# A fused attention and MLP kernel on one core: zeroing moved, dummy matmuls moved to the front, one load freed of a wait, and all written instruction orders replaced

## The chip, the core and the metric

The kernel runs on one core of a Trainium2 chip. Its time is the device time of one execution in microseconds; the figure for a kernel is the median of several executions. The engines are TensorE (PE in the profile, its weight loads PEld), VectorE (DVE), ScalarE (ACT), GpSimd (POOL) and SyncE (SP). Matrix products go to PSUM; a "tile" below is a named buffer in on-chip memory.

## The reference

Eight batches of eight heads, 576 rows, width 64, go through a Nyström approximation of attention with 32 landmarks, and the result through an MLP with a squared ReLU.

```python
q_lm = q.reshape(B, H, m, S // m, D).mean(axis=3)      # m = 32 landmarks
k_lm = k.reshape(B, H, m, S // m, D).mean(axis=3)
A, Bm, C = sm(q, k_lm), sm(q_lm, k_lm), sm(q_lm, k)    # softmax(scale * a @ b.T)
Z = Bm.T / (norm1(Bm) * norminf(Bm) + 1e-6)
for _ in range(6):
    Z = 2 * Z - Z @ Bm @ Z                             # iterative inverse
x = (A @ Z @ C @ v)                                    # to (4608, 512)
out = np.maximum(x @ w_in, 0) ** 2 @ w_out             # w_in 512x2048, w_out 2048x512
```

## The kernel before

The work is done batch by batch. For a batch the kernel copies k and q to bf16 (tile nat), transposes them (T, and tT for the last 64 rows), takes the landmark means as matmuls against a constant matrix seg (L344), puts them on block diagonals (bd), and computes the landmark scores (L374), their softmax (BB), and the iterative inverse as a chain of small products (L416) and VectorE updates (L421). Scores of q and k against the landmarks (L532, with their tails in L560) are exponentiated by ScalarE into EA and EC. EA is normalised (row sums L574, an in L586) and transposed to AT (L598). C times v is gathered in L616. The MLP's first matrix is folded in: G is the small attention factor times w_in (L807), so that the hidden layer h is one product of G with AT (L824); ScalarE applies ReLU (r, L828), VectorE squares (gT, L829), and L853 multiplies by w_out, in 36 tiles of 16 matmuls of 512 columns, followed by copies o_sb and stores.

The first batch, called the head, has no MLP work to hide behind. Its order is the string HEAD; a last product az and its copy AZ stand in for AT there. The other batches are interleaved with the MLP of the batch before, by the eight strings in PLANS: PLANS[b] holds the hidden layer of batch b, the attention of batch b + 1 and output steps. Both are written orders: in the block of `tc.manual_schedule` the instructions of PE, DVE, ACT and SP go out exactly as the tokens say. POOL's order is set by `issue_after` chains and added dependencies.

The tokens that matter here: `ck` casts k to bf16 by halves (VectorE half 0 at L719, ScalarE half 1 at L720) and starts the remaining loads; `tk0`, `tk1`, `tq0`, `tq1` transpose halves, `ek..`, `eq..` copy them out on the engine named by the last letter; `cq0`, `cq1` copy the halves of q; `mk`, `mq` are means; `lm`, `ls` the landmark scores and their softmax; `ib`, `if` begin the inverse, `jo`, `jl`, `nu`, `nn`, `fv` are its steps; `sq`, `sk`, `tl` scores and tails; `sum`, `rec`, `row` normalise EA; `cv`, `cr`, `cba`, `ct` handle C times v; `g:n` makes a quarter of G and `gf`, `gl` copy it out; `w:n:width` issues n dummy matmuls of that width into a tile idle nobody reads (L297, 512 columns without a width), from the zeroed constant bd1. In a plan, `h` is one hidden block, `s` a squaring, a number that many output steps, `pk`, `pq` the copy of k or q of the next batch (L283; with `+` of the batch after it, which starts its transposes on the DMA engines for batches from 3 on), `gg` half of G.

Loads go out from POOL one behind the other (`load`, `behind`), except the first k on SP. `load_rest`, called in `ck`, issues the loads listed in LOADS (parts of w_in, w_out, v, and q and k of batch 1, whose landing place is the tile stage). The first of them is made to wait, through `gate`, for the ScalarE cast of k. Behind these loads POOL copies one part of seg and zeroes two tiles ct, 128 x 1280 bf16 each. ct is read only by batches from DMA_C = 9 on, and there are eight batches; likewise DMA_A = 9 for a transposing DMA of an.

Of the kernel before, what the change touches and what calls it, by code (L numbers as in the profile page):

```python
# [9 lines left out]
P = 128  # L10
# [4 lines left out]
BF16 = mybir.dt.bfloat16  # L15
# [12 lines left out]
NC4 = 4  # L28
# [5 lines left out]
DMA_C = 9  # L34
COMPACT = 1
HEAD = (
    "ck tk1 mk w:1:256 w:1:256 ek1d w:1:256 w:1 tk0 tt w:1 w:1 cq0 cq1 ek0a mq tq0 tq1 lm "
    "w:1 et w:1:256 w:1 eq0a w:1:256 tl eq1d ls sum:0:4:5 w:1 ib w:1 w:1:256 sq1 w:1:256 if "
    "sk1 sum:1:2:5 w:1:256 w:1 sum:1:0:2 jo w:1:256 w:1:256 rec:1 w:1:256 row:1:0:3 "
    "row:1:3:5 w:1:256 sk0 w:1 sq0 jo w:1:256 w:1:256 w:1 w:1:256 sum:0:2:4 sum:0:0:2 w:1 jo "  # L40
    "rec:0 cv:0 cv:1 w:1:256 w:1:256 row:0:3:5 cr jo w:1:256 row:0:0:3 w:1:256 at:1 cba w:1 "
    "jl at:0 ea0d ea1a ct w:1:256 nu w:1:256 g:0 gl1d fv w:1 gf1d w:1 gf0a az gl0d"
)
LOADS = "w10 v0 w00 q1 w01 w11 o0 o1 o2 o3 v1"
PLANS = [
    (
        "pk h g:1 tt h pq h s tk1 s h s h tq1 s tk0 h h mk s s mq tq0 h lm s g:2 g:3 ls sk0 s h "
        "h ib 1 h 1 s if tl h jo 1 sq0 s 1 jo s s 1 h jo 1 sq1 1 jl h 1 nu h s s h nn 2 sk1 nu s "
        "1 s 8 as0 1 ar0 as1 2 ar1 5 nn1 cv 4 wt at0 2 gg0 2 at1 2 gg1 1"
    ),  # L50
    (
        "2 pk 1 h h 1 mk pq s mq 1 s h tq0 lm h ls h tt tq1 3 tl 1 s 1 h ib 1 s if s sq1 2 s h "
        "jo 1 as1 sq0 1 h h s 1 as0 tk1 1 jo 1 s 4 tk0 2 jo 1 h 1 s h 1 pk+ 1 jl ar1 h sk0 1 s 1 "
        "s nu h s 1 sk1 s h h nn s cv nu h 3 nn1 at1 s 3 s wt 3 ar0 2 gg0 3 at0 1 gg1 pq+"
    ),
    (
        "5 mk h 1 h mq s 2 h 5 lm s 2 ls 1 sk1 2 ib 3 h h s sk0 s if 1 s h 2 h 1 jo s h tl 3 jo "
        "1 s 2 h jo 1 s 2 h 3 s sq0 s 1 jl pk+ 4 sq1 2 as0 nu 3 h 1 nn 2 as1 1 pq+ 1 nu 1 h 1 "
        "ar1 h 1 s s h 1 nn1 cv 1 h 2 ar0 1 s wt h 1 at0 2 gg1 1 s at1 1 s 2 gg0 1 s"
    ),  # L60
    (
        "mk 2 h 1 mq 7 h 2 s lm s 1 ls 1 h sq1 1 h h 1 ib 1 s if sk1 1 s h s 2 h jo 1 s 1 h s 1 "
        "jo 2 h 1 pk+ jo 1 tl s h 2 jl as1 sq0 1 s h 1 s h nu s 1 h sk0 s 1 ar1 4 as0 nn 1 ar0 2 "
        "h 3 cv 2 s h nu 4 s nn1 1 at1 1 h wt 2 s 3 s gg1 1 at0 4 gg0 4 pq+"
    ),
    (
        "2 mk h 2 mq 4 h lm 1 h 1 s ls 1 sk0 s ib s 3 h h if 3 tl s 2 h h s 1 s jo 2 h h 1 jo s "
        "1 sq0 s 2 h 1 jo 5 s 10 jl pk+ s 3 sq1 h nu 1 h 1 h 3 as0 sk1 s 1 h 1 as1 ar1 5 s nn cv "
        "nu pq+ 4 s 2 nn1 ar0 h s 4 wt h 2 at0 s 1 gg0 2 s 1 at1 1 gg1 2"
    ),  # L70
    (
        "3 mk mq 3 h lm 3 h h ls 1 s 1 s ib 2 sq1 h 2 if 1 sq0 3 jo h 1 sk0 s jo 2 s h jo tl 4 "
        "as1 1 h 1 jl s sk1 h 3 pk+ s 4 nu h 1 s 2 s 1 s 4 as0 h 1 ar1 nn s 2 ar0 h cv h nu h s "
        "1 s 1 nn1 h 2 h pq+ s wt h 2 at1 2 gg0 at0 5 s 3 s s gg1"
    ),
    (
        "mk 1 mq 3 h s lm 1 h 3 ls 2 h s 1 ib 2 h 1 if sq1 s h 1 s 3 sq0 2 s h 2 s 2 jo h tl 3 "
        "jo 1 h h as0 jo 3 s h 1 s jl 1 s sk1 4 nu 2 as1 h nn 1 h 1 sk0 2 ar0 nu 1 s s 3 h h 1 "
        "cv 2 nn1 s h s 1 at0 1 wt h 2 s 1 ar1 gg0 1 at1 2 s 1 gg1 4 s"
    ),  # L80
    (
        "h 7 h 6 s 1 h 6 h 1 s 2 h s 2 h 6 s 13 h 2 s 2 h 1 s 1 s 5 s h 3 h 1 s s h 11 s 1 h s 8 "
        "h 1 h 1 h 1 s 4 s h 2 s s"
    ),
]

# [2 lines left out]
def kernel(  # L89
# [9 lines left out]
    nc = tc.nc  # L99

    const = ctx.enter_context(tc.tile_pool(name="const", bufs=1))
# [19 lines left out]
    vts, ects, cts = [], [], []  # L121
# [5 lines left out]
        nc.vector.memzero(ect[:])  # L127
        ects.append(ect)

    behind, gate = [], []  # L130

    def load(dst, src, queue=nc.gpsimd):
        with tc.issue_after(behind[0].ins) if behind else nullcontext():
            d = queue.dma_start(dst, src)  # L134
        if gate:
            tc.add_manual_dep(
                d.ins, gate.pop().ins.name,
                mybir.DependencyInfo(mybir.DependencyClass.Sync, mybir.DependencyReason.DATA),
                reason="q first")
        if queue is nc.gpsimd:  # L140
            behind[:] = [d]
        return d
# [18 lines left out]
    def load_qk(b: int, X: dict):  # L161

        X["qkt"] = loads.tile([P, H, D], BF16, tag="qkt", name="qkt")

        def tails():
            for src, r0 in ((k, k_row(b)), (q, q_row(b))):
                load(X["qkt"][r0:r0 + TAIL, :, :],
                     src[b, :, NC4 * P:S, :].rearrange("h p d -> p h d"))

        if b > 0:  # L170
            tails()
        for nm, src in (("k", k), ("q", q)):
            if b < 3:
                X[nm + "raw"] = staged(b, nm)
            else:
                X[nm + "raw"] = loads.tile([P, H, NC4, D], BF16, tag="raw", name="raw")
            parts = ((0, H // 2), (H // 2, H)) if b == 0 and nm == "q" else ((0, H),)
            for lo, hi in parts:
                one = load(
                    X[nm + "raw"][:, lo:hi, :, :],  # L180
                    src[b, lo:hi, 0:NC4 * P, :].rearrange("h (p c) d -> p h c d", c=NC4),
                    nc.sync if b == 0 and nm == "k" else nc.gpsimd)
                if b > 0 and nm + "turn" in loaded[b - 1]:
                    tc.add_manual_dep(
                        one.ins, loaded[b - 1][nm + "turn"].ins.name,
                        mybir.DependencyInfo(mybir.DependencyClass.Sync,
                                             mybir.DependencyReason.DATA),
                        reason="behind the turning of the batch before")
            if b == 0 and nm == "k":
                tails()  # L190

# [10 lines left out]
    loaded = {b: {} for b in range(B)}  # L202
# [6 lines left out]
    seg = const.tile([P, NC4 + 3, M], BF16, name="seg")  # L209
# [21 lines left out]

    EA = const.tile([P, 2, NC4 + 1, P], F32, name="EA")
    nc.vector.memset(EA[:, :, NC4, :], 1.0)

    def load_rest(after):

        def w_in(i, j):
            load(
                w_in_bf[64 * i:64 * i + 64, :, 1024 * j:1024 * j + 1024],
                moe_w_in[256 * i:256 * i + 256, 1024 * j:1024 * j + 1024].rearrange(  # L240
                    "(j d) f -> d j f", d=D),
            )

        def w_out(j):
            load(
                w_out_bf[:, 4 * j:4 * j + 4, :],
                moe_w_out[512 * j:512 * j + 512, :].rearrange("(ft fp) c -> fp ft c", fp=P),
            )

        behind[:] = [masked]  # L250
        gate[:] = [after]
        for x in LOADS.split():
            i = int(x[1])
            if x[0] == "w":
                w_in(i, int(x[2]))
            elif x[0] == "o":
                w_out(i)
            else:
                (load_v if x[0] == "v" else load_qk)(i, loaded[i])
        with tc.issue_after(behind[0].ins):  # L260
            nc.gpsimd.tensor_copy(seg[:, NC4 + 2, :], seg[:, NC4, :])
            for i in range(2):
                ct = const.tile([P, 2, NC4 + 1, P], BF16, name="ct%d" % i)
                nc.gpsimd.memset(ct[:], 0.0)
                cts.append(ct)

    turn = [0]

# [31 lines left out]
    def attention(b: int, R: dict):  # L300

        X = loaded[b]
        BD = bds[b % 2]
        ect = ects[b % 2]
        first = b == 0
# [193 lines left out]
        ct = cts[b % 2] if b >= DMA_C else None  # L499
        c0 = b % 2  # L500
        at = NC4 * (1 - c0)
# [10 lines left out]
        an = attn.tile([P, 2, NC4 + 1, P], BF16, tag="an", bufs=1, name="an")  # L512
        AT = attn.tile([P, 2, (NC4 + 1) * P], BF16, tag="AT", name="AT")
# [76 lines left out]

        def a_transposed(i):
            if b >= DMA_A:
                nc.sync.dma_start_transpose(AT[:, i, :].rearrange("p (c t) -> p c t", t=P),
                                            an[:, i, :, :].rearrange("p c x -> p (c x)"))
                return
            tps = ntile([P, (NC4 + 1) * P], BF16, placed=b > 0)
            for c in range(NC4 + 1):
                nc.tensor.transpose(tps[:, c * P:c * P + P], an[:, i, c, :], ident_bf[:])  # L598
            o = TAIL * c0
            return AT[:, i, o:o + S], tps[:, o:o + S]  # L600
# [110 lines left out]
        def head_step(token):  # L711
# [5 lines left out]
            if name == "ck":  # L717
                raw = natural(0, "k")
                dve(X["k"][:, 0:2], raw[:, 0:2])  # L719
                load_rest(act(X["k"][:, 2:4], raw[:, 2:4]))  # L720
                st["qraw"] = natural(0, "q")
                X["tT"] = attn.tile([P, NPAIR, P], BF16, tag="tT", name="tT")
            elif name[:2] == "cq":
# [252 lines left out]
```

The softmax here doesn't subtract the row's maximum and nothing guards it: scores larger than these inputs give would overflow.

## Time and profile before

| what | value |
|---|---|
| median of 7 runs | 266.14 us (265.54 to 266.64) |
| the profiled execution: time, span | 266.22 us, 264.5 us |
| PE busy | 247.9 us, 94% |
| DVE busy | 176.7 us, 67% |
| ACT busy | 158.3 us, 60% |
| POOL busy | 47.7 us, 18% |
| first PE instruction | 7.67 us |
| first h matmul (L824) | 25.07 us |

The span runs from the first to the last recorded instruction; the profiled execution is 1.72 us longer than it. A row of the timeline reads: start, duration, engine, line, operation, output tile <- input tiles, shapes, count, and in brackets the idle time of the engine before it with what ended it. Matmul records carry the latency of a matmul, so matmuls that follow each other overlap in them.

### The profile page before, as it was taken

The page shows a single profiled execution, that of the slowest core. Times are in us where ns is not written, and L with a number is a line of the kernel's source. Part 1 is how long each engine was busy: PE and PEld are TensorE (multiplying, and loading weights), DVE is VectorE, ACT ScalarE, POOL GpSimd, SP SyncE. Part 2 cuts the span into 40 slices and gives each one's busy share as a digit, 9 for nine tenths or more (in the row PEclk, how much of TensorE's full clock was granted, in tenths as well). Part 3 has the DMA queues.
Part 4 walks back from the last instruction along what each step waited for, and adds up shares of the span by engine and source line. Part 5 has one row for each costly group of instructions (what it writes and reads, how often), then busy time and mean ns, then how long its engine had stood idle before and what let it go on. Part 6 is the DMA issues. An engine that isn't in the chain of part 4 may idle for free.

```text
span 264.5 us, 6918 instructions
## 1 busy us (share of the span) xinstructions
PE 247.9 (94%) x2835; PEld 153.4 (58%) x2878; DVE 176.7 (67%) x485; ACT 158.3 (60%) x278; POOL 47.7 (18%) x73
## 2 busy tenths in 40 slices
PE   0898899999999999999999999999999999999994
PEld 0675665467656656566556565666566655555443
DVE  3488986789985878689767589589776783232100
ACT  2464787279666765678557566674777665365210
POOL 7844633302010500700003101230000000000000
PEclk9999999999999999999999999999999999999999
DMA  8999999997149899996838998999911111112122
GB/s 189 163 192 203 208 206 190 212 208 102 37 95 191 112 194 161 180 205 129 121 79 112 182 184 108 127 176 197 161 51 40 42 40 69 52 40 83 40 79 79
DMA packets 69791, 34.65 MB, mean 131 GB/s; under 512 B 37376, under 2 KB 64256, under 8 KB 69760
## 3 DMA queue, kind: packets, MB, share of 16 engines
q0 software_dynamic: 39808, 17.83, 54.2%
q1 hardware_dynamic: 24704, 7.08, 17.4%
q10 hardware_dynamic: 5248, 9.31, 11.3%
q8 instruction: 22, 0.36, 0.6%
q14 instruction: 9, 0.07, 0.1%
HBM read 36.70 MB, written 9.44 MB: 174 GB/s over the span
## 4 chain that ended last, share of the span: by engine, by line
PE 87%; DVE 5%; DMA 2%; issue 2%; ACT 2%; ACTq 0%
PE ops L853 24%; PE h L824 22%; PE n L853 21%; PE n L532 3%; PE g L807 3%; PE idle L297 2%; DMA stage<-in_k_dram 2%; PE n L416 2%; PE n L344 2%; PE n L598 2%; PE n L616 1%; DVE nat L283 1%; DVE gT L829 1%; PE tps L315 1%; PE n L631 1%
## 5 line engine op out<-in xcount | busy, mean ns | idle before, releaser
L828 ACT ACTIVATE r<-h 128x576 bf16<-128x576 f32 x128 | 81.2, 651 | 46.7 <-PE h L824 33.9
L853 PE MATMUL ops<-w_out_bf,gT 128*128 128x512 bf16 (+1 forms) x300 | 76.8, 368 | 0.9 <-issue 0.3
L853 PEld LDWEIGHTS <-gT 128*128 128x128 bf16 x592 | 53.2, 98 | 38.7 <-issue 4.2
L829 DVE TENSOR_TENSOR gT<-r 128x576 bf16<-128x576 bf16 x128 | 54.8, 447 | 26.3 <-ACT r L828 26.1
L824 PE MATMUL h<-AT,G 128*128 128x288 bf16 x448 | 71.0, 286 | 0.2
L853 PE MATMUL n<-w_out_bf,gT 128*128 128x512 bf16 x252 | 69.7, 379 | 1.1 <-issue 0.3
L824 PEld LDWEIGHTS <-G 128*128 128x128 bf16 x512 | 47.7, 97 | 24.3 <-issue 0.8
L705 DVE CAST G<-g 128x1024 bf16<-128x1024 f32 x14 | 17.1, 1224 | 5.4 <-PE g L807 5.4
L864 ACT COPY o_sb<-ops 128x512 f32<-128x512 f32 (+1 forms) x19 | 10.9, 574 | 14.5 <-PE ops L853 14.5
L864 ACT COPY o_sb<-n 128x512 f32<-128x512 f32 x17 | 10.0, 586 | 12.9 <-PE n L853 12.8
L705 ACT CAST G<-g 128x1024 bf16<-128x1024 f32 x14 | 14.2, 1014 | 4.5 <-PE g L807 4.5
L134 POOL DMA_DIRECT2D raw<-in_k_dram x5 | 4.5, 890 | 54.2 <-DVE gT L829 28.4
L532 PEld LDWEIGHTS <-T 128*128 128x128 bf16 x256 | 11.3, 98 | 4.2 <-issue 0.6
L574 DVE TENSOR_REDUCE ra<-EA 128x20 f32<-128x640 f32 (+3 forms) x19 | 13.2, 703 | 0.3 <-ACT EA L562 0.3
L586 DVE TENSOR_TENSOR an<-EA,rra 128x640 bf16<-128x640 f32 (+2 forms) x18 | 13.2, 736 | 0.2
L532 PE MATMUL n<-bd,T 128*128 128x64 bf16 x256 | 12.7, 193 | 0.3 <-issue 0.2
L315 PEld LDWEIGHTS <-nat 128*128 128x128 bf16 x96 | 6.6, 106 | 9.8 <-ACT nat L720 7.7
L537 ACT ACTIVATE EA<-n 128x512 f32<-128x512 f32 x16 | 9.6, 598 | 3.3 <-PE n L532 3.2
L134 POOL DMA_DIRECT2D raw<-in_q_dram x5 | 4.4, 884 | 38.8 <-DVE rc L447 27.7
L537 ACT ACTIVATE EC<-n 128x512 bf16<-128x512 f32 x16 | 9.5, 596 | 3.0 <-PE n L532 1.6
L824 PE MATMUL h<-AZ,G 128*128 128x288 bf16 x64 | 10.0, 286 | 0.6 <-DVE AZ L797 0.4
L315 PE MATMUL tps<-ident_bf,nat 128*128 128x128 bf16 x32 | 3.1, 266 | 7.7 <-ACT nat L720 7.7
(144 smaller groups left out, 294.8 us busy)
## 6 DMA issues: line engine op xcount, KB each, us to landing
out_dram<-o_sb ACTq DMA_DIRECT2D x31, 256.0 KB, 3.5
vm<-in_v_dram POOLq DMA_DIRECT2D x8, 512.0 KB, 10.2
raw<-in_k_dram POOLq DMA_DIRECT2D x5, 512.0 KB, 6.9
raw<-in_q_dram POOLq DMA_DIRECT2D x5, 512.0 KB, 6.9
w_in_bf<-in_moe_w_in_dram POOLq DMA_DIRECT2D x4, 512.0 KB, 12.3
w_out_bf<-in_moe_w_out_dram POOLq DMA_DIRECT2D x4, 512.0 KB, 17.4
out_dram<-o_sb ACTq DMA_DIRECT2D x9, 128.0 KB, 2.4
stage<-in_k_dram SPq DMA_DIRECT2D x1, 1024.0 KB, 5.7
```

Of the source, the lines that this page charges most:

```text
L134: d = queue.dma_start(dst, src)
L315: nc.tensor.transpose(tps[:, i, p, :], X[nm][:, 2 * half + i, 2 * p:2 * p + 2, :].rearrange("p h d -> p (h d)"), ident_bf[:],)
L532: nc.tensor.matmul(sc[:, c, j, :, :], lhsT=X[nm + "T"][:, c, p, :], rhs=BD[:, 1 if nm == "q" else 0, p, 0:64], start=True, stop=True)
L537: nc.scalar.activation(dst, sc.rearrange("p c j i m -> p c (j i m)"), AF.Exp, scale=SCALE)
L574: nc.vector.reduce_sum(ra[:, quads, lo:hi, :], EA[:, quads, lo:hi, :].rearrange("p q c (h m) -> p q c h m", m=M), axis=AX.X)
L586: on.tensor_tensor(an[:, i, lo:hi, :].rearrange("p c (h m) -> p c h m", m=M), EA[:, i, lo:hi, :].rearrange("p c (h m) -> p c h m", m=M), r ...
L705: (act, dve)[n % 2](G[:, :, n * 512:n * 512 + 512], gg[:])
L824: nc.tensor.matmul(h[:, j, 0:HALF], lhsT=G[:, qd, f * P:(f + 1) * P], rhs=AT[:, qd, a0 + j * HALF:a0 + (j + 1) * HALF], start=(qd == 0), s ...
L828: nc.scalar.activation(r.rearrange("p (j t) -> p j t", j=2), h[:, :, 0:HALF], AF.Relu)
L829: return lambda: nc.vector.tensor_tensor(gT[:, f, o:o + S], r[:], r[:], ALU.mult)
L853: nc.tensor.matmul(ops, lhsT=gT[:, f, t * P:t * P + P], rhs=w_out_bf[:, f, i * n:i * n + n], start=(f == 0), stop=(f == NF - 1))
L864: nc.scalar.copy(o_h, ops)
```

## The change

It does five things. Sixteen dummy matmuls of 512 columns open TensorE's order. ct is zeroed by VectorE at the start, and the part of seg is copied by VectorE too. The wait of the first load of `load_rest` (gate) is taken out. HEAD and all eight PLANS are replaced by new orders of the same steps, with 13 dummies behind the first 16 where there were 35; some steps also change engine (`ek0` from ScalarE to VectorE, `ek1` from VectorE to ScalarE, and so on). A load of k would also wait for the transposing DMAs of `a_transposed` two batches earlier, if there were any.

```diff
 HEAD = (
-    "ck tk1 mk w:1:256 w:1:256 ek1d w:1:256 w:1 tk0 tt w:1 w:1 cq0 cq1 ek0a mq tq0 tq1 lm "
-    "w:1 et w:1:256 w:1 eq0a w:1:256 tl eq1d ls sum:0:4:5 w:1 ib w:1 w:1:256 sq1 w:1:256 if "
-    "sk1 sum:1:2:5 w:1:256 w:1 sum:1:0:2 jo w:1:256 w:1:256 rec:1 w:1:256 row:1:0:3 "
-    "row:1:3:5 w:1:256 sk0 w:1 sq0 jo w:1:256 w:1:256 w:1 w:1:256 sum:0:2:4 sum:0:0:2 w:1 jo "
-    "rec:0 cv:0 cv:1 w:1:256 w:1:256 row:0:3:5 cr jo w:1:256 row:0:0:3 w:1:256 at:1 cba w:1 "
-    "jl at:0 ea0d ea1a ct w:1:256 nu w:1:256 g:0 gl1d fv w:1 gf1d w:1 gf0a az gl0d"
+    "w:16 ck tk0 w:1 ek0d w:1:256 tk1 w:1 cq0 mk cq1 tt w:1 et ek1a mq tq0 lm eq0d tl ls tq1 "
+    "w:1 ib eq1a w:1:256 if sq1 sum:0:4:5 jo sq0 sum:1:2:5 sum:1:0:2 sk1 jo rec:1 sum:0:2:4 "
+    "w:1:256 sk0 sum:0:0:2 w:1 w:1:256 jo cv:0 cv:1 row:1:0:3 jo rec:0 cr row:1:3:5 cba "
+    "row:0:3:5 w:1 w:1 row:0:0:3 ct at:1 jl w:1 ea1a at:0 nu ea0d fv g:0 gf1d gf0a az gl0a "
+    "w:1 gl1a"
 )
...
 PLANS = [
     (
-        "pk h g:1 tt h pq h s tk1 s h s h tq1 s tk0 h h mk s s mq tq0 h lm s g:2 g:3 ls sk0 s h "
-        "h ib 1 h 1 s if tl h jo 1 sq0 s 1 jo s s 1 h jo 1 sq1 1 jl h 1 nu h s s h nn 2 sk1 nu s "
-        "1 s 8 as0 1 ar0 as1 2 ar1 5 nn1 cv 4 wt at0 2 gg0 2 at1 2 gg1 1"
+        "pk h tt s h g:1 pq s tk1 h h tk0 tq1 h mk s mq h s s tq0 lm ls h h s sq1 g:2 g:3 ib s h "
+        "h if s sk0 1 h jo 1 s 1 s sq0 jo s h 1 jo h jl tl s s h 1 nu 2 as1 ar1 sk1 h 1 h s 1 nn "
+        "at1 2 nu 2 s s 11 as0 2 ar0 1 nn1 cv 4 wt 1 at0 1 gg0 5 gg1 3"
     ),
...
-    behind, gate = [], []
+    behind = []
...
-        if gate:
-            tc.add_manual_dep(
-                d.ins, gate.pop().ins.name,
-                mybir.DependencyInfo(mybir.DependencyClass.Sync, mybir.DependencyReason.DATA),
-                reason="q first")
...
-                if b > 0 and nm + "turn" in loaded[b - 1]:
-                    tc.add_manual_dep(
-                        one.ins, loaded[b - 1][nm + "turn"].ins.name,
...
+                turns = [] if b == 0 else [loaded[b - 1].get(nm + "turn")]
+                if b > 1 and nm == "k":
+                    turns += loaded[b - 2].get("aturn", [])
+                for turn in turns:
+                    if turn is not None:
+                        tc.add_manual_dep(
+                            one.ins, turn.ins.name,
...
     nc.vector.memset(EA[:, :, NC4, :], 1.0)
-
-    def load_rest(after):
+    for i in range(2):
+        ct = const.tile([P, 2, NC4 + 1, P], BF16, name="ct%d" % i)
+        nc.vector.memset(ct[:], 0.0)
+        cts.append(ct)
+    nc.vector.tensor_copy(seg[:, NC4 + 2, :], seg[:, NC4, :])
+
+    def load_rest():
...
         behind[:] = [masked]
-        gate[:] = [after]
...
-        with tc.issue_after(behind[0].ins):
-            nc.gpsimd.tensor_copy(seg[:, NC4 + 2, :], seg[:, NC4, :])
-            for i in range(2):
-                ct = const.tile([P, 2, NC4 + 1, P], BF16, name="ct%d" % i)
-                nc.gpsimd.memset(ct[:], 0.0)
-                cts.append(ct)
...
-                load_rest(act(X["k"][:, 2:4], raw[:, 2:4]))
+                act(X["k"][:, 2:4], raw[:, 2:4])
+                load_rest()
```

## The prediction

> **What bounds the kernel now.** I read the page first: the engine totals, then the chain that ended last.
>
> ```profile
> span 264.5 us, 6918 instructions
> PE 247.9 (94%) x2835; PEld 153.4 (58%) x2878; DVE 176.7 (67%) x485; ACT 158.3 (60%) x278; POOL 47.7 (18%) x73
> ...
> PE 87%; DVE 5%; DMA 2%; issue 2%; ACT 2%; ACTq 0%
> PE ops L853 24%; PE h L824 22%; PE n L853 21%; PE n L532 3%; PE g L807 3%; PE idle L297 2%; DMA stage<-in_k_dram 2%; PE n L416 2%; PE n L344 2%; PE n L598 2%; PE n L616 1%; DVE nat L283 1%; DVE gT L829 1%; PE tps L315 1%; PE n L631 1%
> ```
>
> TensorE is busy in 94% of the span and holds 87% of the chain; most of that is the MLP (L824, L853), which the change leaves alone. It is idle for only 16.6 us (264.5 - 247.9), so I asked where, with the busy time by stretch (columns: length, then busy time of PE, weight load, DVE, ACT, POOL).
>
> ```profile
> 0.00:7.67 7.67, 0.00 (x0) 0.00 (x1) 3.51 (x15) 2.33 (x2) 5.18 (x18) 1.00 0.96 189
> 25.05:50.00 24.95, 23.12 (x341) 14.74 (x345) 21.14 (x50) 17.66 (x34) 11.06 (x14) 1.00 1.36 202
> 50.00:240.00 190.00, 187.42 (x2083) 115.19 (x2114) 137.30 (x375) 123.50 (x213) 20.35 (x26) 1.00 0.80 123
> 240.00:261.00 21.00, 20.76 (x118) 11.44 (x118) 2.72 (x6) 6.28 (x11) 0.00 (x0) 1.00 0.20 69
> ```
>
> 7.67 us go before TensorE's first instruction, 3.5 at the end behind the last matmul, and 2.58 in the 190 us between 50 and 240. So the steady part has almost nothing to give. What can give is the head, from 7.67 to the first h matmul at 25.07, where TensorE looks busy but the chain counts 2.2% (5.8 us) of dummies (tile idle), and the stretch 25 to 50, with 1.83 us idle. The timeline of the head shows two speeds.
>
> ```profile
> 7.67 1.03 PE L315 MATMUL tps<-ident_bf,nat 128*128 128x128 bf16 x8 [7.67 <-ACT nat L720]
> 11.38 1.06 PE L297 MATMUL idle<-bd 128*128 128x512 bf16 x2
> 12.79 1.05 PE L315 MATMUL tps<-ident_bf,nat 128*128 128x128 bf16 x16
> ```
>
> Eight transposes take 1.03 us at 7.67 and sixteen take 1.05 at 12.79. The clock column reads 1.00 everywhere, so it does not show this; the durations do. In the timeline of the stretch behind the head one more thing stands out.
>
> ```profile
> 25.60 0.68 DVE L283 COPY nat<-stage 128x2048 bf16<-128x2048 bf16 x1
> ...
> 27.19 2.28 POOL L264 MEMSET ct<- 128x1280 bf16 x2
> 27.19 2.83 DVE L283 COPY nat<-stage 128x2048 bf16<-128x2048 bf16 x1
> ...
> 30.08 1.07 PE L315 MATMUL n<-ident_bf,nat 128*128 128x128 bf16 x16 [0.96 <-DVE nat L283]
> ```
>
> The same copy takes 0.68 us for k and 2.83 for q, and the long one starts and ends with the two memsets of ct on POOL. TensorE waits 0.96 us for it.
>
> **What the Trainium skill says.** "TensorE: Matmul & The Clock Gate", section "What's actually happening", has TensorE at half clock until it has been busy for about 3.4 us, and again after an idle window as long. The trace agrees on the half speed; full speed came near 12.4, 4.7 us after the first matmul. "SBUF — State Buffer", section "SBUF: two separate sides", says that VectorE in its two-port copy mode and GpSimd take turns on one port pair, and the loser blocks for a whole instruction: it agrees, 2.83 against 0.68 us. "VectorE: DVE Perf Modes", section "Zero memsets can be issued as uint32 (trn2)": one cycle per element, so a zeroed bf16 tile costs half its elements. The trace has 128x512 uint32 x2 in 1.02 us, 1 ns per element.
>
> **Part by part.** (1) 16 dummies of 512 columns now open TensorE's order. They need only bd1, zeroed by 1.5. At the cold spacing of 0.42 us (11.38 to 11.80) all 16 would last to 8.3; if the clock rises 4.7 us after their start (6.3), eleven are cold and five warm (0.22 us each), and they end at 7.35. The first transposes move from half 1 of k (cast by ScalarE, ready 7.62) to half 0 (VectorE, ready 7.26). So real work starts at 7.4 and warm.
>
> (2) The head in its new order, walked with the durations of this trace, each step at the later of its inputs and its engine. Eight warm transposes 0.55, dummies 0.3, eight more 0.5, dummy 0.2, k means (20 at 0.03) 0.6: k means done 9.65. The second half of q lands at 9.95 (issue 3.56 plus 6.4), its copy ends 10.45 and the q means 10.9. ScalarE still has the 1.01 us copy of T ahead of its bd copy, so the landmark scores start at 11.6, against 13.68 before. Exp, row sums, BB and the copy of T on VectorE give EY at 14.35 (16.89 before). The four joint steps end on VectorE at 14.95, 16.15, 17.35, 18.15 (before 17.95, 19.26, 20.17, 21.21), each behind a row sum or a row product. Then the gain shrinks: four normalising operations (rc and three rows, 0.15 + 0.43 + 0.43 + 0.55) stand ahead of y, which ends at 20.2 (22.12 before). v is done at 21.45 (23.94 before) and the first h starts at about 22.65 (25.07 before). Head: 2.4 us less. Dummies fall from 35 (21 of 256 columns, 14 of 512) to 13 behind the first 16; in the walk those cover waits, so their removal is already in the 2.4 and is not counted twice. Bounds: 1.6 if each queue hand-over costs 0.05 more than I took, 3.0 if the rows slip beside the products.
>
> (3) ct moves from POOL to VectorE's first list: 640 uint32 each, 0.65 us, two make 1.3 us, from 3.5 to 4.8. VectorE waits there 3.08 us for k (6.57), so this is free; if k landed before 4.8 it would cost up to 1.3. POOL issues loads meanwhile; it took 0.70 to 0.81 us for each beside the memsets it meets now, as later, so I charge it nothing. The copy of seg also goes to VectorE, behind the k cast; its input on POOL is done by 5.8, so it delays blk and the evacuation of T by 0.1 at most. On POOL 2.3 us of memsets and the seg copy are gone, and the q copy falls back to 0.68: VectorE gets 2.15 us and TensorE most of its 0.96 wait. I take 0.9, bounds 0 (something else late at once) and 1.2 (its weight load waited 1.27).
>
> (4) The first w_in load no longer waits 1.50 us for ScalarE's cast. POOL can issue it at 6.4 for 7.91, and v0, w00 and the tails behind it move as much. The DMA rate falls to 57 GB/s between 9 and 10 against 170 to 197 around it, so the stream gains the hole, about 0.7 us, not 1.5. Nothing in the head waited for these loads, so I cost it at nothing; its value is that the loads keep up. With 0.7 off, k1 lands at 22.7 and q1 at 25.4 (23.4 and 26.1 now, issue plus landing); their copies are reached at 23.0 and 25.4. The last w_in part lands at 30.4 (31.1) and is used from 31.0; w_out's first part lands at 33.5 and is used from 33.6. No slack over 0.6, but no wait. If q were slowed by the earlier w_in, each 0.1 us would be 0.1 us of head.
>
> (5) All eight plans are written anew. The set of MLP matmuls is the same (506 output steps inside the plans in both), so only idle time and hand-overs can change: 2.58 us idle in 50 to 240, of which a better order could save perhaps 1 and a worse one add as much or more. I take zero, bounds -1 and +2.6 (doubled). I followed each copy of k and q that starts transposes (pk+, pq+) to its use and each load to the copy that frees its buffer; the closest, q of the last batch, has some 6 us left. The added wait on aturn never arises: DMA_A is 9, no batch reaches it.
>
> The sum against the profiled execution, 264.5 span + 1.72 around it = 266.22: 266.22 - 2.4 - 0.9 = 262.9. The median of 266.14 lies 0.08 below that execution, too little to correct for.
>
> **Rivals.** Transfers set the pace: the loads come 0.7 us earlier, the head 2.4, and k1, q1, w_in and w_out are nearly late at once. DMA moves 190 to 217 GB/s without pause from 10 to 60, which speaks for it; against it, nothing waited for a load after 7.67. Then the gain is 0.7 plus 0.9: 264.6. The plans lose: the steady idle doubles, +2.6, giving 265.5; against it, every stretch from 50 to 240 stays near 0.4 us idle per 25 to 30 us. On the other side, the clock falls back: behind the opening block the dummies stream 5,632 columns instead of 12,544, and TensorE waits for VectorE between products. If it went cold at 12, some 5 us of TensorE's steps on the chain would take twice as long (+5), and 4.7 us at half speed would follow at the start of the MLP (+2.35): 262.9 + 7.35 = 270.3. It decides once TensorE's idle share lets the skill's window count as idle; against it, the walk has no gap above 0.7 us. That the change does not do what it says is excluded by the two instruction orders, except that ct is never read (DMA_C is 9): only the move off POOL counts.
>
> **How the numbers follow.** The forecast has 0.67, its own range 261.2 to 264.3; transfers 0.13; plans that lose 0.08; the clock 0.08; 0.04 for anything else. Changes below 0.2% (0.53 us) cannot be told from none by a measurement of this kernel. The plans rival falls half in "same"; the rest of "same" and of "slower" is the last 0.04. Faster 0.84, same 0.05, slower 0.11. The range takes in the transfers and most of the plans rival, and on the low side a steady part better by 1 with a head of 3.0: 260.7 to 265.9.
>
> **What would show it.** First real transposes near 7.4 at 0.55 us for eight; landmark scores (L374 before) near 11.6; first h near 22.65; both nat copies at 0.68 us; TensorE idle about 0.9 us less between the first h and 25 us after it; the steady 190 us the same within 1. Wrong if transposes behind the opening block still take 1.03 us for eight, if a wait for nat, w_in or w_out on DMA appears, or if PE idle in the steady part grows by over 2 us.

## The result and the profile after

The changed kernel takes 262.77 us (median of 12 runs, 262.27 to 264.46) against 266.05 for the kernel before (31 runs): a ratio of 0.9887, with a 95% interval of 0.9871 to 0.9903. The profiled execution has a span of 261.0 us, 3.5 less. The page of the changed kernel, engine totals and chain:

```profile
span 261.0 us, 6906 instructions
PE 250.3 (96%) x2828; PEld 152.1 (58%) x2872; DVE 176.0 (67%) x486; ACT 159.0 (61%) x280; POOL 45.7 (17%) x70
...
PE 88%; DVE 5%; ACT 4%; issue 2%
```

TensorE is busy for 2.4 us more in a span 3.5 us shorter. The extra is the opening dummies: they fill 6.14 us of what was an idle start, and what TensorE does behind them takes 3.7 us less. The first line of the busy time by stretch shows it (columns: stretch, length, then busy time of PE, weight load, DVE, ACT and POOL, granted clock, DMA share, GB/s). The stretch from the first h matmul on for 25 us, and the steady part behind it, are the other two.

```profile
0.00:7.67 7.67, 6.14 (x16) 2.29 (x17) 4.70 (x18) 2.33 (x2) 6.44 (x20) 1.00 0.96 191
22.20:47.20 25.00, 23.94 (x357) 15.36 (x362) 19.34 (x52) 19.02 (x37) 9.43 (x12) 1.00 1.35 202
50.00:240.00 190.00, 187.68 (x2052) 114.82 (x2085) 137.08 (x373) 123.94 (x215) 20.39 (x26) 1.00 0.75 122
```

In the 25 us behind the first h TensorE is idle for 1.06 us. In the kernel before it was 1.81, in this stretch:

```profile
25.07:50.07 25.00, 23.19 (x344) 14.79 (x348) 21.18 (x51) 17.64 (x34) 11.06 (x14) 1.00 1.36 202
```

In the steady 190 us TensorE is idle for 2.32, before 2.58. The timeline of the changed kernel's head:

```profile
1.53 6.38 PE L293 MATMUL idle<-bd 128*128 128x512 bf16 x16 [1.53 <-DVE bd L116]
...
7.75 0.61 PE L311 MATMUL tps<-ident_bf,nat 128*128 128x128 bf16 x8
...
11.59 0.27 PE L370 MATMUL n<-STk,bd 128*128 128x32 bf16 x4
...
19.45 0.22 DVE L417 SCALAR_TENSOR_TENSOR y<-EY,n 128x64 bf16<-128x64 bf16 x1
...
22.20 0.65 PE L822 MATMUL h<-AZ,G 128*128 128x288 bf16 x4 [0.43 <-DVE AZ L795]
22.34 0.68 DVE L279 COPY nat<-stage 128x2048 bf16<-128x2048 bf16 x1
...
25.27 0.69 DVE L279 COPY nat<-stage 128x2048 bf16<-128x2048 bf16 x1 [0.16 <-DMA stage<-in_q_dram]
```

Eight transposes now take 0.61 us where they took 1.03. The landmark scores start at 11.59 (13.68 before), the first h at 22.20 (25.07), and both nat copies are short. VectorE now waits 0.16 us for the load of q ahead of its copy; TensorE waits for no load behind the first h. From the first h to TensorE's end there are 235.15 us (22.20 to 257.35) where there were 235.79 (25.07 to 260.86): of the 3.51 us, 2.87 come from the head and 0.64 from behind it.

### The profile page after: what moved, and what is told of

It reads as the page before. It is cut to its first block, busy times and chain, and to the rows that moved or that the text cites. A ratio compares the mean times of both kernels' runs of the same rounds, so it can differ in the third digit from the quotient of the medians.

```text
span 261.0 us, 6906 instructions
## 1 busy us (share of the span) xinstructions
PE 250.3 (96%) x2828; PEld 152.1 (58%) x2872; DVE 176.0 (67%) x486; ACT 159.0 (61%) x280; POOL 45.7 (17%) x70
## 4 chain that ended last, share of the span: by engine, by line
PE 88%; DVE 5%; ACT 4%; issue 2%
PE ops L851 23%; PE h L822 22%; PE n L851 21%; PE g L805 3%; PE idle L293 3%; PE n L340 3%; PE n L528 3%; PE n L412 2%; PE n L595 2%; DVE gT L827 1%; PE n L613 1%; PE n L311 1%; PE n L628 1%; PE tps L311 1%; ACT G L642 1%
## 5 line engine op out<-in xcount | busy, mean ns | idle before, releaser
L822 PEld LDWEIGHTS <-G 128*128 128x128 bf16 x512 | 47.0, 97 | 21.4 <-ACT AZ L795 0.4
L293 PE MATMUL idle<-bd 128*128 128x512 bf16 (+1 forms) x25 | 9.2, 497 | 1.7 <-DVE bd L116 1.5
L340 PEld LDWEIGHTS <-nat 128*128 128x128 bf16 x256 | 8.3, 96 | 2.4 <-DVE nat L723 0.3
L412 PEld LDWEIGHTS <-ED 128*128 128x128 bf16 x72 | 6.3, 98 | 5.6 <-DVE EY L451 1.2
```

The costliest lines, as they stand in the source:

```text
L293: nc.tensor.matmul(idle[:, 0:width], lhsT=z[:, 0:P], rhs=z[:, 0:width], start=True, stop=True)
L340: nc.tensor.matmul(means[:, ti, p, :], lhsT=src.rearrange("p h d -> p (h d)"), rhs=seg[:, c + (ti if c == NC4 else 0), :], start=(n == 0 a ...
L822: nc.tensor.matmul(h[:, j, 0:HALF], lhsT=G[:, qd, f * P:(f + 1) * P], rhs=AT[:, qd, a0 + j * HALF:a0 + (j + 1) * HALF], start=(qd == 0), s ...
```

## The experiments

The theory was that three edits and the new head order each bring a part: the clock is up when work begins, the q copy no longer meets POOL, and the head's order uses what the clock gives. The rivals were that loads set the pace, that the new plans lose or win, and that the clock falls back. The ratio beside each is to the kernel before on the same chip, with its 95% interval.

### One edit at a time on the kernel before

**ct and the part of seg on VectorE.**

```diff
+    for i in range(2):
+        ct = const.tile([P, 2, NC4 + 1, P], BF16, name="ct%d" % i)
+        nc.vector.memset(ct[:], 0.0)
...
+    nc.vector.tensor_copy(seg[:, NC4 + 2, :], seg[:, NC4, :])
...
-            nc.gpsimd.tensor_copy(seg[:, NC4 + 2, :], seg[:, NC4, :])
...
-                nc.gpsimd.memset(ct[:], 0.0)
```

> The kernel before, all orders kept, with only ct and the part of seg moved from POOL to VectorE. Theory (the two memsets hold the copy of q, and TensorE waits for it): the q copy (L283 before) falls from 2.83 to about 0.68 us, TensorE's idle time in the 25 us behind the first h falls by about 0.9 us, first h stays at 25.1, time 265.2 against 266.1. Rival (something else is late at once): the copy is short but the time stays at 266.0 or more. Rival (the early memsets delay the casts of k): first h later by up to 1.3 us.

264.79 us against 265.66, ratio 0.9966 (0.9945 to 0.9987). Its timeline and its stretch behind the first h:

```profile
27.25 0.69 DVE L282 COPY nat<-stage 128x2048 bf16<-128x2048 bf16 x1
```

```profile
25.13:50.13 25.00, 24.10 (x358) 15.67 (x363) 19.75 (x53) 17.56 (x34) 8.50 (x11) 1.00 1.35 201
```

The copy is short, the first h has not moved (25.13), and TensorE is idle 0.90 us where it was 1.81. So 0.9 us are gained by taking POOL out of the copy's way, and nothing else was late at once. ct and the part of seg were moved together; which of them would have been enough was not tried.

**The opening dummies.**

```diff
-    "ck tk1 mk ...
+    "w:16 ck tk1 mk ...
```

> The kernel before with only the 16 dummies of 512 columns put in front of TensorE's order. Theory (the clock rises before the real work): the first eight transposes take about 0.6 instead of 1.03 us, q's means end near 11.2 instead of 12.9 because the second half of q lands at 9.95, first h near 23.7 instead of 25.07, time 264.8. Rival (the head is held by q and the VectorE queue, not by TensorE's speed): first h moves by less than 0.5, time 265.7 or more. Rival (16 dummies outlast the cast of k): first transposes later than 8.0.

263.86 us, ratio 0.9922 (0.9902 to 0.9942), more than expected. Timeline of the opening and the head's end:

```profile
1.53 6.55 PE L297 MATMUL idle<-bd 128*128 128x512 bf16 x16 [1.53 <-DVE bd L117]
7.92 0.61 PE L315 MATMUL tps<-ident_bf,nat 128*128 128x128 bf16 x8
...
23.49 0.65 PE L824 MATMUL h<-AZ,G 128*128 128x288 bf16 x4 [0.41 <-DVE AZ L797]
...
26.80 0.69 DVE L283 COPY nat<-stage 128x2048 bf16<-128x2048 bf16 x1 [0.77 <-DMA stage<-in_q_dram]
```

The head is 1.58 us shorter. The q copy is short too, though ct stays on POOL: it is over at 27.49, and POOL begins its own copy of seg at 27.76. So part of ct's gain is counted here as well, and the parts don't simply add. The copy of q now waits 0.77 us for its load, and TensorE is idle for 1.30 us in the 25 us behind the first h (23.70 busy): with the shorter head of this trace the loads are no longer early enough.

**The wait of the first w_in load.**

```diff
-        gate[:] = [after]
```

> The kernel before with only the wait of the first w_in load on the cast of k taken out. Theory (nothing in the head waits for these loads): first w_in issue near 6.4 instead of 7.9, k1 and q1 land about 0.7 us earlier, time 266.1, no change within 0.2%. Rival (loads set the pace behind the head): 0.5 to 0.7 us faster. Rival (w_in slows q): first h later by some tenths, slower.

265.71 us, ratio 1.0021 (0.9994 to 1.0048): nothing that can be told, as the theory said. Four of its 14 executions, though, took 267.0 to 268.4 us, above the highest of the kernel before on that chip (266.87 in 23), and what held them isn't known. The first w_in issue is at 6.36, and k1 (the k of batch 1) lands 0.9 us earlier (POOL's wait for it ends at 22.88, against 23.74). One thing in its timeline is odd:

```profile
26.48 2.41 POOL L260 COPY seg<-seg 128x32 bf16<-128x32 bf16 x1
26.49 2.35 DVE L282 COPY nat<-stage 128x2048 bf16<-128x2048 bf16 x1
28.84 2.25 POOL L263 MEMSET ct<- 128x1280 bf16 x2
```

Here the q copy is long beside POOL's small copy of seg, and the memsets run after it, alone. In the kernel before that small copy was short and over when the long one had hardly begun:

```profile
27.05 0.22 POOL L261 COPY seg<-seg 128x32 bf16<-128x32 bf16 x1
```

Its first h is at 24.38, 0.7 earlier, which fits a clock that rose sooner in this execution (the second eight transposes, at 10.37, take 0.73 us); the median shows nothing of it.

**The three edits together**, with the orders of before (the first lines of the three diffs above):

```diff
-    "ck tk1 mk ...
+    "w:16 ck tk1 mk ...
...
+        nc.vector.memset(ct[:], 0.0)
...
-        gate[:] = [after]
```

> The kernel before with the three edits together (16 dummies in front, ct on VectorE, no wait of the first w_in load) and its own HEAD and PLANS otherwise. Theory (parts add): 266.1 - 0.9 - 1.3 = 263.9, first h near 23.7. The new orders then bring the last 1.1 us. Rival (the new orders bring nothing, the edits all): 262.8. Rival (the parts hide each other, loads late once the head is short): 264.8 or more, with waits for stage, w_in or w_out.

263.37 us, ratio 0.9904 (0.9882 to 0.9927), first h at 23.58. Once k is there, neither TensorE, VectorE nor ScalarE waits for a load ahead of the first h in its trace. The copy of q no longer waits for its load either, and the idle time in the 25 us behind the first h is 0.89 us, against 1.30 with the dummies alone. That fits a freed load that is worth some tenths once the head is shorter, though ct was moved here too. Most of the whole gain is here without any new order: it lies between the theory's 263.9 and the rival's 262.8.

### The two halves of the new orders

Both have the three edits and one half of the new orders: first the new HEAD with PLANS of before, then HEAD of before (with w:16) and the new PLANS. The third is the changed kernel unedited.

```diff
-    "w:16 ck tk1 mk w:1:256 w:1:256 ek1d ...
+    "w:16 ck tk0 w:1 ek0d w:1:256 tk1 w:1 ...
```

> The changed kernel with the eight PLANS of the kernel before: three_edits with the new HEAD alone. Theory (the new orders pay in the head; the plans bring nothing or cost a little: from the first h to TensorE's end the trace has 235.15 us with the new plans and 234.72 in three_edits): first h at 22.2, 1.4 us less than three_edits, the rest 234.7, so 0.4 us below the changed kernel. Rival (the new plans fit the new head, and the old ones lose behind it, with k1 and q1 nearly late): 0.5 us or more above the changed kernel, with waits for stage in 22 to 26.

```diff
-        "pk h g:1 tt h pq h s tk1 ...
+        "pk h tt s h g:1 pq s tk1 ...
```

> three_edits with the new PLANS alone. Theory: first h near 23.6 as in three_edits, 0.4 us above three_edits (263.4). Rival (the new plans save about half a microsecond): 262.9 or less.

> The changed kernel itself, for comparison on the same chip: first h near 22.2, 0.989 of the kernel before.

On one chip these took 262.71 us (0.9887, 0.9857 to 0.9916), 263.42 (0.9919, 0.9889 to 0.9949) and, for the changed kernel itself, 262.77 (0.9899, 0.9861 to 0.9936). First h: 22.75, 23.54 and 21.93; from there to TensorE's end: 234.69, 234.63 and 234.80 us. The plans make no difference that can be seen, with either head; neither the 0.4 us that I expected them to cost nor the rival's 0.5 gained showed. The new head gives 0.6 to 0.7 us, at the edge of what these intervals separate; the traces support it, since the gain sits ahead of the first h in both pairs. One trace gives the first h only roughly, though: that of one and the same head lay between 21.93 and 22.75 in three executions.

### Taking parts out of the changed kernel

**No opening dummies.**

```diff
-    "w:16 ck tk0 w:1 ek0d ...
+    "ck tk0 w:1 ek0d ...
```

> The changed kernel without the 16 opening dummies, the 13 others kept. Theory (the new head needs the early clock as much as the old one): first eight transposes about 1.0 us from 7.3, first h 1.3 to 2 us later than 22.2, time 264.2 to 265. Rival (the head's gain is the new order's alone, limited by q and VectorE): first h within 0.5 of 22.2, time 263.2 or less.

263.57 us, ratio 0.9920 (0.9898 to 0.9942): 0.8 above the changed kernel, at the edge of what the intervals separate, and between the two expectations. Timeline:

```profile
7.26 1.03 PE L311 MATMUL tps<-ident_bf,nat 128*128 128x128 bf16 x8 [7.26 <-DVE nat L716]
...
12.78 0.31 PE L370 MATMUL n<-STk,bd 128*128 128x32 bf16 x4
```

The transposes are slow again and the scores 1.2 us late, first h 0.96 us late (23.16). In the old head the opening dummies moved it by 1.58 us. Whether the new head needs the early clock less isn't shown: these are single executions, and the old head's first h without dummies was at 25.07 in one and at 24.38 in another (gate_only).

**No late dummies.**

```diff
-    "w:16 ck tk0 w:1 ek0d w:1:256 tk1 w:1 cq0 mk cq1 tt w:1 et ...
+    "w:16 ck tk0 ek0d tk1 cq0 mk cq1 tt et ...
```

> The changed kernel with only the 16 opening dummies; the 13 behind them are left out (9 of 512 columns, 4 of 256). Theory (they cover waits or cost a little, the clock stays up without them): first h 0.1 to 0.5 us earlier than 22.2, time 0.1 to 0.5 below the changed kernel, transposes and score matmuls at their warm latencies (219 and 193 ns). Rival (the clock falls back): latencies of 128-column matmuls near 312 ns somewhere between 12 and 30, and 2 us or more slower.

264.14 us, ratio 0.9940 (0.9921 to 0.9959): 1.4 slower than the changed kernel. The rival is right in what happens, though its 2 us or more is too much for the median. All 13 executions had a mean granted clock of 0.993 or less (0.968 in the profiled one, the slowest); of the changed kernel's 18, 15 had 0.997 or more. Its timeline, and the busy time by stretch, whose third column from the end is the granted clock:

```profile
11.14 0.36 PE L340 MATMUL n<-seg,nat 128*128 128x32 bf16 x8 [1.35 <-DVE nat L723]
12.03 0.27 PE L370 MATMUL n<-STk,bd 128*128 128x32 bf16 x4
12.14 0.59 PE L556 MATMUL n<-bd,tT 128*128 128x128 bf16 x4
```

```profile
8.00:10.00 2.00, 1.79 (x47) 1.57 (x44) 1.58 (x6) 0.58 (x3) 2.00 (x4) 1.00 1.34 209
10.00:12.00 2.00, 0.86 (x18) 0.70 (x18) 1.35 (x3) 1.12 (x2) 2.00 (x4) 0.97 1.15 201
12.00:14.00 2.00, 2.00 (x20) 2.00 (x20) 1.65 (x6) 1.36 (x4) 1.23 (x2) 0.50 1.46 199
26.00:28.00 2.00, 2.00 (x18) 1.01 (x17) 1.24 (x3) 1.16 (x3) 0.06 (x1) 0.50 1.12 210
28.00:30.00 2.00, 2.00 (x21) 1.62 (x19) 1.48 (x3) 1.76 (x4) 0.62 (x1) 0.77 1.20 204
```

TensorE waits 1.35 us for the second half of q, whose load came late in this execution (VectorE waited 0.81 us for it). From 12 to about 29 the clock is at half, and the first h comes at 24.30. TensorE is slower in that time and VectorE isn't. Here are TensorE's product az and VectorE's row products, the first two lines from the changed kernel and the other two from this one:

```profile
21.10 0.67 PE L790 MATMUL az<-AT,v 32*32 32x288 bf16 x16
18.29 1.21 DVE L582 TENSOR_TENSOR an<-EA,rra 128x256 bf16<-128x256 f32 x3
...
22.98 1.14 PE L790 MATMUL az<-AT,v 32*32 32x288 bf16 x16
19.64 1.21 DVE L582 TENSOR_TENSOR an<-EA,rra 128x256 bf16<-128x256 f32 x3
```

So the late dummies are no filling: they keep the clock.

**ct on POOL again**, in the changed kernel.

```diff
-        nc.vector.memset(ct[:], 0.0)
...
-    nc.vector.tensor_copy(seg[:, NC4 + 2, :], seg[:, NC4, :])
...
+            nc.gpsimd.tensor_copy(seg[:, NC4 + 2, :], seg[:, NC4, :])
...
+                nc.gpsimd.memset(ct[:], 0.0)
```

> The changed kernel with ct and the part of seg back on POOL behind the loads. Theory (the stall needs a copy of nat to meet the memsets; in the new order POOL reaches them at about 26.4, after the copy of q at 25.3): no copy of nat over 0.8 us, time equal to the changed kernel within 0.3 us. Rival (memsets on POOL cost VectorE and TensorE 0.9 us wherever they stand): 263.6 or more.

262.58 us, ratio 0.9898 (0.9864 to 0.9931), not slower than the changed kernel. But six of its eight runs took 262.4 to 262.8 and two 264.0, and the profiled one is of the longer kind. Its timeline:

```profile
25.26 2.85 DVE L280 COPY nat<-stage 128x2048 bf16<-128x2048 bf16 x1
25.75 2.41 POOL L258 COPY seg<-seg 128x32 bf16<-128x32 bf16 x1
28.11 2.25 POOL L261 MEMSET ct<- 128x1280 bf16 x2
```

So the theory's median holds and its picture doesn't: POOL reached the seg copy at 25.75, inside the q copy, and the meeting cost 2.2 us of VectorE as before. TensorE is idle 2.14 us in the 25 us behind the first h (22.86 busy). I take it that the other six executions missed the meeting; they weren't profiled. Where it is missed, moving ct brings nothing that can be told on top of the other edits.

**The wait of the first w_in load put back**, in the changed kernel.

```diff
+        gate[:] = [after]
```

> The changed kernel with the wait of the first w_in load on the cast of k put back. Theory (with the short head q1 arrives just in time, so 0.7 us of load time is now worth something): the copy of q1 waits 0.6 to 0.9 us for its load instead of 0.16, first h unchanged at 22.2, time 0.3 to 0.7 above the changed kernel. Rival (still hidden): equal within 0.2 us.

264.56 us, ratio 0.9938 (0.9917 to 0.9960): 1.8 above the changed kernel, where I expected 0.3 to 0.7 and an unmoved first h. The waits of TensorE in its head, and two lines of its timeline:

```profile
PE n L619 <- DMA vt<-in_v_dram: 1.2, 1, 1.2
```

```profile
16.73 0.30 PE L619 MATMUL n<-vm,EC 128*32 128x64 bf16 x16 [0.20 <-ACT EC L539]
18.24 0.21 PE L619 MATMUL n<-vt,ect 128*32 128x64 bf16 x4 [1.20 <-DMA vt<-in_v_dram]
```

The load that is late is the tail of v, which I had not placed: it was issued at 9.72 and took 8.5 us. In the changed kernel it is issued at 8.30, lands at 15.9 and is used from 16.85. The wait that I expected isn't there: the copy of q1 waits for no load in this trace. Behind the idle 1.2 us the clock falls, to half from about 20.5 to 27:

```profile
18.00:20.00 2.00, 1.56 (x49) 1.04 (x49) 1.18 (x6) 0.32 (x2) 0.75 (x1) 1.00 1.69 174
20.00:22.00 2.00, 1.68 (x42) 1.08 (x39) 1.32 (x4) 1.06 (x3) 1.64 (x3) 0.61 1.48 198
22.00:24.00 2.00, 1.67 (x26) 0.74 (x27) 1.48 (x4) 1.19 (x4) 0.71 (x2) 0.50 1.46 199
```

The first h comes at 23.97. The single executions split the 1.8 us: the 8 of 22 executions that kept a mean clock of 0.997 or more took 263.3 us in the median, against 262.7 for the 15 such executions of the changed kernel, and the other 14 took 263.8 to 266.1. So the wait itself seems to cost about half a microsecond, and the rest goes with the fallen clock; only one of the 22 was profiled.

### More dummies

```diff
-    "... tt w:1 et ... if sq1 ... jo cv:0 ... row:0:3:5 w:1 w:1 ... at:0 nu ea0d fv g:0 gf1d ...
+    "... tt w:1 w:1:256 et ... if w:1:256 sq1 ... jo w:1:256 cv:0 ... row:0:3:5 w:1 w:1 w:1 w:1 ...
+    ... at:0 w:1:256 nu ea0d w:1:256 fv g:0 w:1:256 gf1d ...
```

> The changed kernel with nine dummies more (seven of 256 columns, two of 512) at places where TensorE waits for another engine in the head. Theory (the changed kernel loses its full clock in some executions, since the 13 late dummies are barely enough): no execution above 263.5, mean granted clock 0.997 or more in all, median 0 to 0.3 below the changed kernel. Rival (dummies delay the chain): first h 0.3 later or more, median above 263.0.

The kernel has eight dummies more, six of 256 columns and two of 512; the expectation miscounts them. It took 263.18 us (0.9915, 0.9884 to 0.9947), 262.74 to 263.69 with a clock of 0.997 or more in all seven runs. Of the changed kernel's 18 runs three were above 264, at mean clocks of 0.985 to 0.991. That fits late dummies that are barely enough in some executions, but seven without a fall don't show it: at a rate of three in 18, chance alone gives that in about one case of four. With the eight the first h comes at 22.61 and the median is 0.4 higher, less than the intervals separate. Both sides were half right, and this is no better version. None of the kernels tried beats the changed one by what the intervals can tell.

## Why the prediction was right

The predicted 262.9 stands against 262.77: opening dummies, head order and the copy of q out of POOL's way are what paid, and the plans paid nothing, as forecast. That the sum fits to 0.1 us is partly luck. In the profiled execution the head gained 0.47 us more than its term and what lies behind it 0.26 less (0.64 against 0.9), and the terms overlap in a way that the sum doesn't have. The terms, in the prediction's own order:

- **Opening dummies.** They end at 7.9, not 7.35: the clock rose some 5.5 us after their start, not 4.7, and real work starts at 7.54. The expected 0.55 for eight transposes measured 0.61. The 4.7 us were one execution's figure; the runs gave 2.8 to 6.0 (last section).
- **The head.** Predicted 2.4, measured 2.87, inside the bounds of 1.6 to 3.0. The walk held nearly to the tenth up to the joint steps: scores 11.6 (11.59), EY 14.35 (14.30), joint updates 14.95, 16.15, 17.35, 18.15 (14.93, 16.09, 17.07, 18.17). The term that was mis-sized is the row normalising ahead of y, which ended at 19.67, not 20.2. The prediction's four operations and y (0.22) add up from 18.15 to 19.93 only, so 0.27 us stand in none of its figures; and three rows one behind the other took 1.21 us, not the sum of 1.41. Everything behind kept about that half microsecond. (The figures for the k means add up to 9.55, not 9.65; nothing hung on it.)
- **ct.** Predicted 0.9; alone on the kernel before it measured 0.9 (median and idle time), in the changed kernel 0.75 of idle time. But it is the price of one meeting, not of ct: the copy of q was short in dummies_only with ct still on POOL, and with ct put back into the changed kernel the median was not higher (262.58) and two of eight executions were. So the earlier head alone mostly avoids the meeting, and part of the 0.9 could have been claimed by either term. The working also named only one partner. In the kernel before the copy did run beside the memsets (27.19 to 30.02; it ended 0.55 us behind them, not with them), but gate_only and ct_on_pool show the same loss beside the small copy of seg, with the memsets behind it. That part moved with ct, so the sum held.
- **The freed load.** Its price of nothing is right for the kernel before (1.0021, 0.9994 to 1.0048) and for the sum, since the other terms were already worked with loads that keep up. The landing times were close: k1 22.5 (predicted 22.7), q1 25.3 (25.4), last w_in 30.5 (30.4), first w_out 33.1 (33.5). But the tail of v was left out of that list, and it was the one with a price: without the edit the new head loses 1.8 us, about 0.5 of it in executions without a fall of the clock. A wait on such a load, named as a sign of being wrong, shows once in the changed kernel, with 0.16 us ahead of the copy of q, and reaches no matmul. That nothing waits for these loads was true of the kernel before alone; with the dummies in front the copy of q already waited 0.77 us.
- **The plans.** Predicted zero; measured zero within the intervals, and 2.32 us of steady idle against 2.58.
- **The rivals.** Transfers set the pace only when the freed load is tied again. The clock's fall is real: the 13 late dummies prevent it in most executions. Its price of 7.35 us (5 in the head, 2.35 behind) was far too high. The profiled no_late_dummies was at half clock over about the stretch that was priced, from 12 to 29, and took 3.2 us more (264.2 span against 261.0): by the first h and the span's end some 1.7 in the head behind the scores, 0.4 ahead of them with the late q, and 1.1 behind the first h. The median execution lost 1.4, at a mean clock of 0.98, by which I estimate some 10.5 us at half clock (0.02 x 262 x 2). The step that was wrong is that TensorE's steps on the chain would take twice as long. Its short products hardly grow: from the start of the first joint product to VectorE's update it was 0.29 us at full clock (14.35 to 14.64) and 0.35 at half (15.42 to 15.77). Only longer ones such as az come near it, and VectorE's steps keep their time. The deciding gap is shorter than I took from the Trainium skill ("TensorE: Matmul & The Clock Gate", section "What's actually happening", an idle window of about 3.4 us): waits of 1.35 us (no_late_dummies) and 1.20 us (wait_back) in stretches of short matmuls were followed by half clock here. That these single waits were the cause isn't shown; in wait_back the clock fell only 2.2 us after the wait had ended.

## What to carry to other kernels

Dummy matmuls in the idle start cost next to nothing here (the first real weight load came at 7.54 us, before at 7.67) and bought the clock for the real work. A few behind them may be what keeps the clock; take them away one group at a time and look at every execution and its granted clock, not at one. When a head is shortened, list every load with its landing and its first use, small tails too, since a wait that cost nothing before becomes the bound. Keep a copy or memset of GpSimd out of the moment at which VectorE makes a large bf16 copy: one of 0.22 us was enough here to stretch a copy of 0.68 to 2.35 us and more.

## What was not expected of the hardware

- The time from TensorE's first matmul to full clock varies between executions. Judged by the spacing of the opening dummies' weight loads (0.43 us cold), it was 2.8 us in three_edits, 3.7 in changed_again, 5.5 in the changed kernel and about 6 in dummies_only. The first two lines are from three_edits (the spacing shrinks at 4.38), the other two from the changed kernel (7.05):

```profile
4.06 0.15 PEld L295 LDWEIGHTS <-bd 128*128 128x128 bf16 x1 [0.28 <-issue]
4.38 1.61 PEld L295 LDWEIGHTS <-bd 128*128 128x128 bf16 x8 [0.16 <-issue]
...
6.62 0.15 PEld L293 LDWEIGHTS <-bd 128*128 128x128 bf16 x1 [0.28 <-issue]
7.05 0.37 PEld L293 LDWEIGHTS <-bd 128*128 128x128 bf16 x2 [0.28 <-issue]
```

  On one chip the kernel before spread over 264.2 to 266.9 us (23 executions), dummies_only over 263.7 to 264.1 (6) and ct_only over 264.3 to 265.3 (10). Both edits seem to narrow it; what share the clock and the copy have in it wasn't settled.
- The profile's clock column reads 1.00 in the cold start (first stretch of the changed kernel, with weight loads 0.43 us apart) and 0.50 after a fall (no_late_dummies, 12 to 14).
- VectorE's 0.68 us copy and GpSimd's 0.22 us copy, begun within 0.5 us of each other, took 2.35 to 2.85 and 2.41 us. The section "SBUF: two separate sides" of the Trainium skill's "SBUF — State Buffer" has one blocked for the other's whole instruction; 0.22 us don't explain 2.2. GpSimd's own spans are rough, but its next issue also came late, at 31.05 in gate_only, 4.57 us after its copy of seg began, against 2.35 (27.05 to 29.40) in the kernel before. What holds both is left open.
